# A static scheduler that lengthens both sides of a shared-port overlap, in a kernel of sparse attention and a squared-ReLU layer

## The chip, the cores and the metric

The kernel runs on one core of a Trainium2 chip. The metric is the device time of one execution of the whole program, in microseconds, as the median of several executions; the span of a profile, from its first to its last instruction, is a little shorter.

Five engines of the core work side by side, each in the order of its own instruction list: TensorE (PE, matmuls), VectorE (DVE), ScalarE (ACT), GpSimd (POOL) and SyncE (SP, which here only issues transfers). They wait for each other by semaphores.

## The reference

The reference computes block-sparse attention on 4 batches of 8 heads, 768 positions of 64 features, and then a two-layer feed-forward on the 3072 resulting tokens of 512 features:

```python
scores = (q @ k.T) / sqrt(64)              # per batch and head, 768 x 768
mask   = abs(block_i - block_j) <= 1       # blocks of 32 positions
mask  |= first or last block, as row or as column
mask  |= 3 sampled key blocks for each query block
attn   = softmax(where(mask, scores, -1e9))
x      = (attn @ v), heads side by side     # 3072 tokens x 512
h      = x @ w_in                           # 512 -> 2048
out    = (max(h, 0) ** 2) @ w_out           # 2048 -> 512
```

## The kernel before

The kernel does not write its instructions in a fixed order. It makes a list of tasks, each with the engines that may run it and an estimated duration on each, the tasks it depends on, and the buffers it takes and gives back. A greedy scheduler then walks through estimated time, and each time places the ready task that can start first; ties go to the lower key. What it places becomes the next instruction of that engine. So the estimates decide the order, and the order is fixed before the program runs. On the chip each engine then follows its list, and waits when an input is not there.

```python
LAT = {"PE": 0.23, "DVE": 0.06, "ACT": 0.06, "POOL": 0.08, "SP": 2.0}
SWITCH = 0.1
AHEAD = {"PE": 0.05, "DVE": 0.2, "ACT": 0.25, "POOL": 0.0, "SP": 0.0}
...
def run_schedule(free, bufs, dma_free, mode=128):
    port = {"DVE": (0.0, 0.0), "POOL": (0.0, 0.0)}
    ...
            for e, us in t.engs.items():
                r = max([r0, free[e]] + [seen(d, e) for d in t.deps])
                sw = SWITCH if e == "PE" and t.mode and t.mode != mode else 0.0
                if e == "POOL" or (e == "DVE" and t.port):
                    p0, p1 = port["DVE" if e == "POOL" else "POOL"]
                    us += 0.7 * max(0.0, min(r + us, p1) - max(r, p0))
                if opt is None or r + us + t.bias.get(e, 0.0) < opt[3] - 1e-9:
                    opt = (r + us + sw, r, e, r + us + t.bias.get(e, 0.0))
            found.append((round(opt[1], 4), t.key, t.order, t, opt))
            if t.key < 100:
                urgent[opt[2]] = min(urgent.get(opt[2], 1e9), opt[1])
        best = min((c for c in found if c[1] < 100 or c[0] + AHEAD[c[4][2]] < urgent.get(c[4][2], 1e9)),
                   key=lambda c: c[:3], default=None)
```

`port` holds the last interval of a task on VectorE that uses the SBUF port it shares with GpSimd, and of one on GpSimd. A task that falls into the other engine's interval is made longer by 0.7 of the overlap. The other task, placed already, keeps its length. Tasks with keys under 100 (attention) are urgent; others may start on an engine only if they start by `AHEAD` before the next urgent one.

One attention step is a query tile of 256 positions against two key chunks of 128, for two heads. It is four tasks:

```python
def scores(slots, add, e):      # TensorE, 8 matmuls of 256 columns with 64 rows (two steps: 16)
    ...
                nc.tensor.matmul(ps[:, h, c, :], QK[i][hs, 1, ksl], QK[i][hs, 0, qsl], ...)
def exps(a, e):                 # ScalarE, 128 x 1024, PSUM to SBUF
    A.activation(out=pT, in_=stile.pop(a), func=AF.Exp, scale=scale)
def masks(a, e):                # VectorE, both inputs in SBUF
    V.tensor_tensor(out=pT, in0=pT, in1=m[:, None].broadcast_to([P, 2, 2, QW]), op=AOP.mult)
def values(a, e):               # TensorE, 8 matmuls of 65 columns into the one bank "po"
    ...
def normalize(u, qi, e):        # VectorE, after three steps; then "po" is free again
    V.reciprocal(out=rs, in_=po[:, :, :, D:VW])
    V.tensor_tensor(out=xq, in0=po[:, :, :, 0:D], in1=rs.broadcast_to([P, 2, 2, D]), op=AOP.mult)
```

A score group is four matmuls a step (two heads, two chunks). The first query tile of batch 0 has its mask added by further matmuls; all other steps multiply by a mask `MK` of zeros and ones, which twelve mask tasks on TensorE make at the start. Loads of later batches are cast to bf16 (`cast_qk` on VectorE or GpSimd, `cast_v` mostly on GpSimd).

The feed-forward works on tiles of 256 or 384 tokens:

```python
def hidden(T, f, half, e):      # TensorE, 4 matmuls of 256 or 384 columns for each of 16 f
def relu(T, f, e):              # VectorE or ScalarE, PSUM to SBUF
    if e == "ACT":
        A.activation(out=r, in_=src, func=AF.Relu)
    else:
        V.tensor_scalar(out=r, in0=src, scalar1=0.0, scalar2=None, op0=AOP.max)
def square(T, f, e):            # GpSimd or ScalarE
    if e == "ACT":
        A.activation(out=g, in_=r, func=AF.Square)
    else:
        (G if e == "POOL" else V).tensor_mul(out=g, in0=r, in1=r)
def output(T, ts, part, e):     # TensorE, 16 matmuls of 512 columns for 128 tokens, in 8 parts
    ...
def out_copy(T, ts, e):         # ScalarE or VectorE, PSUM to SBUF, 128 x 512
def store(T, ts, e):            # SyncE
    sy.dma_start(out=ov[T[0], :, T[1] // P + ts, :], in_=ystile.pop((T, ts)))
...
SQ = {256: {"POOL": 0.613, "ACT": 0.39}, 384: {"POOL": 0.826, "ACT": 0.49}}
rr = T_(RELU[w], 200, relu, t, f, deps=[h1], get=[rb], put=[hb], bias={"ACT": 0.4})
sq_of[x] = T_(SQ[w], n_key, square, t, f, deps=[rr], get=[gb], put=[rb], bias={"ACT": 0.5})
```

A `bias` is a penalty in us that keeps a task from an engine unless the other is later by more than that. Hidden and output tasks fill TensorE while attention waits; when attention is over, only they are left.

Of the kernel before, what the change touches and what calls it, by code (L numbers as in the profile page):

```python
# [12 lines left out]
F32 = mybir.dt.float32  # L13
# [6 lines left out]
P = 128  # L20
# [5 lines left out]
def kernel(  # L26
# [11 lines left out]
    nc = tc.nc  # L38
    B, H, S, D = q.shape
# [11 lines left out]
    QW = 256  # L51
# [7 lines left out]
    NRAW, NPB, QC_BUFS, XQ_BUFS = 4, 6, 5, 4  # L59
# [19 lines left out]
    SWITCH = 0.1  # L79
    AHEAD = {"PE": 0.05, "DVE": 0.2, "ACT": 0.25, "POOL": 0.0, "SP": 0.0}  # L80
    LEAD = 12.0
    PACE0, PACE, SINGLE, MASK_AT = 40.0, 1.6, 1, 12.0
# [18 lines left out]
    def run_schedule(free, bufs, dma_free, mode=128):  # L101
        taken = {name: [] for name in bufs}
        port = {"DVE": (0.0, 0.0), "POOL": (0.0, 0.0)}
        waiting = list(tasks)
        ready = []

        def seen(d, eng):
            late = d.late if d.late is not None else (0.0 if d.eng == eng else LAT[d.eng])
            return d.end + late

        while waiting or ready:
# [6 lines left out]
            for t in ready:  # L118
                r0 = t.after
                ok = True  # L120
                cnt = {}
                for b in t.get:
                    held = taken[b.pool]
                    at = len(held) + cnt.get(b.pool, 0) - bufs[b.pool]
                    cnt[b.pool] = cnt.get(b.pool, 0) + 1
                    if at >= 0:
                        if held[at].holds:
                            ok = False
                            break
                        r0 = max(r0, held[at].free)  # L130
                if not ok:
                    continue
                opt = None
                for e, us in t.engs.items():
                    r = max([r0, free[e]] + [seen(d, e) for d in t.deps])
                    sw = SWITCH if e == "PE" and t.mode and t.mode != mode else 0.0
                    if e == "POOL" or (e == "DVE" and t.port):
                        p0, p1 = port["DVE" if e == "POOL" else "POOL"]
                        us += 0.7 * max(0.0, min(r + us, p1) - max(r, p0))
                    if opt is None or r + us + t.bias.get(e, 0.0) < opt[3] - 1e-9:  # L140
                        opt = (r + us + sw, r, e, r + us + t.bias.get(e, 0.0))
                found.append((round(opt[1], 4), t.key, t.order, t, opt))
                if t.key < 100:
                    urgent[opt[2]] = min(urgent.get(opt[2], 1e9), opt[1])
# [7 lines left out]
            if e == "POOL" or (e == "DVE" and t.port):  # L152
                port[e] = (at, end)
            if e == "PE" and t.mode:
                mode = t.mode
# [292 lines left out]
    def y_pool(T, ts):  # L448
        return "h" if T == TILES[-1] and ts % 2 else "y"

    def output(T, ts, part, e):
        if part == 0:
            pool, tag = (ps_h, "h") if y_pool(T, ts) == "h" else (ps_y, "y")
            ytile[T, ts] = pool.tile([P, d_model], F32, name="py", tag=tag)
        py = ytile[T, ts]
        for f in range(part * NF // NY, (part + 1) * NF // NY):
            nc.tensor.matmul(py, gtile[T, f][:, ts * P:(ts + 1) * P], w_out_sb[:, f, :],  # L457
                             start=(f == 0), stop=(f == NF - 1))

    def out_copy(T, ts, e):  # L460
        ys = work.tile([P, d_model], F32, name="ys", tag="ys", bufs=3)
        copy(e, ys, ytile.pop((T, ts)))
        ystile[T, ts] = ys

    def store(T, ts, e):
        sy.dma_start(out=ov[T[0], :, T[1] // P + ts, :], in_=ystile.pop((T, ts)))
# [61 lines left out]
    def attend(group, add):  # L528
# [7 lines left out]
        for a in group:  # L536
# [9 lines left out]
            va = T_(("PE", 0.245), s + 2.2, values, a, deps=[ex] + cv[u] + va_all[-1:],  # L546
# [25 lines left out]
    for us in [range(b * HP, (b + 1) * HP) for b in range(B)]:  # L572
# [3 lines left out]
        if us[0] < HP:  # L576
            for c0, c1, at in ((QW, S, MASK_AT), (0, QW, 26.0)):
# [23 lines left out]
    for k_, T in enumerate(TILES + [None]):  # L601
        hs = [(T, f) for f in range(NF)] if T else []
        ys = [(TILES[k_ - 1], ts, part) for ts in range(TILES[k_ - 1][2] // P) for part in range(NY)] if k_ else []
        both = [((i + 0.5) / len(hs), 0, x) for i, x in enumerate(hs)]
        both += [((i + 0.5) / len(ys), 1, x) for i, x in enumerate(ys)]
        for _, kind, x in sorted(both, key=lambda z: z[:2]):
# [3 lines left out]
            if kind == 0:  # L610
# [10 lines left out]
                rr = T_(RELU[w], 200, relu, t, f, deps=[h1], get=[rb], put=[hb], bias={"ACT": 0.4})  # L621
                sq_of[x] = T_(SQ[w], n_key, square, t, f, deps=[rr], get=[gb], put=[rb], bias={"ACT": 0.5})
            else:
                _, ts, part = x
                fs = range(part * NF // NY, (part + 1) * NF // NY)
                if part == 0:
                    yb = Buf(y_pool(t, ts))
                last_ts = ts == w // P - 1
                yy = T_(("PE", 0.432), n_key, output, t, ts, part,
                        deps=[sq_of[t, f] for f in fs] + [wl[NWP + f * NWP // NF] for f in fs] + ([yprev] if part else []),  # L630
                        get=[] if part else [yb], put=[gbuf[t, f] for f in fs] if last_ts else [], mode=128)
                yprev = yy
                if part == NY - 1:
                    sb = Buf("ys")
                    yc = T_({"ACT": 0.585, "DVE": 0.68}, 150, out_copy, t, ts, deps=[yy], get=[sb], put=[yb])
                    T_(("SP", 0.2), 0, store, t, ts, deps=[yc], put=[sb], late=2.0)

    run_schedule({"PE": 5.6, "DVE": 5.6, "ACT": 5.5, "POOL": 5.2, "SP": 12.0},
                 {"ps": 2, "po": 1, "h": 2, "y": 1, "pT": PT_BUFS, "r": R_BUFS, "g": G_BUFS, "ys": 3,
# [31 lines left out]
```

The softmax here doesn't subtract the row's maximum and nothing guards it: scores larger than these inputs give would overflow.

## Time and profile before

The median of three runs is 281.56 us (281.35 to 282.2). The profiled execution has a span of 279.6 us with TensorE's clock at full speed throughout.

| Group (line of the kernel) | Engine | Count | Busy, us | Mean of one, ns |
|---|---|---|---|---|
| hidden matmuls (L427) | TensorE | 576 | 107.8 | 308 |
| output matmuls (L457) | TensorE | 384 | 103.5 | 379 |
| values matmuls (L382) | TensorE | 1152 | 56.5 | 194 |
| scores matmuls (L349) | TensorE | 576 | 46.5 | 272 |
| exponentials (L359) | ScalarE | 144 | 139.2 | 1021 |
| rectifiers (L434) | ScalarE | 64 | 27.3 | 451 |
| squares (L443) | ScalarE | 37 | 18.1 | 489 |
| mask products (L366) | VectorE | 132 | 105.1 | 815 |
| rectifiers (L436) | VectorE | 80 | 41.9 | 525 |
| squares (L445) | GpSimd | 107 | 94.5 | 889 |
| copies of the output (L170) | ScalarE | 21 | 12.3 | 586 |

In lines of the profile, L followed by a number is a line of the kernel. A line of waits reads: who waited, for whom, then the total in us, how often, and the longest. In a line of the order of time the start comes first, then the duration, both in us, then engine, line, operation, output and inputs, and how many instructions were merged; in brackets stands how long the engine had been idle and what ended it. Matmul durations are pipelined and their ends are modelled.

### The profile page before, as it was taken

The numbers are of one execution on the slowest core, as the hardware profiler recorded it, in microseconds if no ns is written. First come the engines' busy times: TensorE is split into PE (matmuls) and PEld (weight loads), VectorE is DVE, ScalarE is ACT, GpSimd is POOL, SyncE is SP. The second block draws the span as 40 slices with busy tenths as digits, with TensorE's granted clock in tenths as the row PEclk, the third lists the DMA queues.
The fourth block names the chain that finished last, engine by engine and source line by source line (L and its number), as shares of the span: only waits on it lengthen the run. The fifth ranks groups of instructions, "written<-read, shape, count | busy, mean of one in ns | idle before, by whom it ended". The sixth has DMA issues, their size and how long they took to land.

```text
span 279.6 us, 7039 instructions
## 1 busy us (share of the span) xinstructions
PE 267.9 (96%) x2834; PEld 155.6 (56%) x2834; DVE 200.4 (72%) x379; ACT 196.5 (70%) x281; POOL 122.1 (44%) x151
## 2 busy tenths in 40 slices
PE   7888899999999998999999999999999999999994
PEld 2565566566666554555555555555556555555541
DVE  6776889898988779986877888877868744344400
ACT  4689889899899799798988889889789501001011
POOL 4570358576434359752114443211120366666610
PEclk9999999999999999999999999999999999999999
DMA  7999997999933784794106314321011010111112
GB/s 249 378 228 207 269 277 239 195 285 258 357 65 83 237 193 120 213 191 106 56 12 115 81 45 111 70 59 49 19 51 56 12 47 38 40 39 38 40 74 76
DMA packets 50379, 36.89 MB, mean 132 GB/s; under 512 B 30891, under 2 KB 47275, under 8 KB 50347
## 3 DMA queue, kind: packets, MB, share of 16 engines
q1 hardware_dynamic: 44762, 30.29, 40.7%
q0 software_dynamic: 4224, 4.19, 9.0%
q10 hardware_dynamic: 1360, 1.97, 2.1%
q8 instruction: 22, 0.36, 0.6%
q14 instruction: 11, 0.08, 0.1%
HBM read 27.26 MB, written 6.29 MB: 120 GB/s over the span
## 4 chain that ended last, share of the span: by engine, by line
PE 78%; DVE 15%; ACT 4%; issue 2%; ACTq 0%; DVEq 0%
PE py L457 27%; PE ph L427 25%; PE po L382 12%; PE ps L349 11%; DVE pT L366 8%; DVE qc L172 3%; ACT pT L359 2%; DVE xq L391 2%; PE junk L213 2%; DVE rs L389 1%; DVE QK L172 1%; PE pt L301 1%; PE ps L353 0%; DVE r L436 0%; DVE xT L172 0%
## 5 line engine op out<-in xcount | busy, mean ns | idle before, releaser
L445 POOL TENSOR_TENSOR g<-r 128x384 bf16<-128x384 f32 (+1 forms) x107 | 94.5, 889 | 128.8 <-DVE r L436 93.0
L359 ACT ACTIVATE pT<-ps 128x1024 bf16<-128x1024 f32 x144 | 139.2, 1021 | 10.8 <-PE ps L349 7.6
L366 DVE TENSOR_TENSOR pT<-pT,MK 128x1024 bf16<-128x1024 bf16 x132 | 105.1, 815 | 9.0 <-ACT pT L359 8.7
L427 PE MATMUL ph<-xT,w_in_sb 128*128 128x384 bf16 (+1 forms) x576 | 107.8, 308 | 0.0
L457 PE MATMUL py<-w_out_sb,g 128*128 128x512 bf16 x384 | 103.5, 379 | 0.0
L427 PEld LDWEIGHTS <-w_in_sb 128*128 128x128 bf16 x576 | 51.1, 97 | 33.3 <-issue 3.4
L436 DVE TENSOR_SCALAR r<-ph 128x384 f32<-128x384 f32 (+1 forms) x80 | 41.9, 525 | 32.9 <-PE ph L427 22.2
L382 PEld LDWEIGHTS <-pT 128*128 128x128 bf16 x1152 | 45.8, 98 | 28.9 <-DVE pT L366 10.9
L382 PE MATMUL po<-VT,pT 128*128 128x65 bf16 x1152 | 56.5, 194 | 3.2 <-DVE pT L366 1.2
L457 PEld LDWEIGHTS <-g 128*128 128x128 bf16 x384 | 34.4, 98 | 25.7 <-issue 1.5
L170 ACT COPY ys<-py 128x512 f32<-128x512 f32 x21 | 12.3, 586 | 50.2 <-PE py L457 50.0
L349 PE MATMUL ps<-QK 64*128 64x256 bf16 x576 | 46.5, 272 | 1.0 <-ACT pT L359 0.8
L349 PEld LDWEIGHTS <-QK 64*128 64x128 bf16 x576 | 22.9, 94 | 21.2 <-issue 17.0
L434 ACT ACTIVATE r<-ph 128x384 f32<-128x384 f32 (+1 forms) x64 | 27.3, 451 | 6.7 <-PE ph L427 6.2
L443 ACT ACTIVATE g<-r 128x384 bf16<-128x384 f32 (+1 forms) x37 | 18.1, 489 | 6.4 <-DVE r L436 5.8
L391 DVE TENSOR_TENSOR xq<-po,rs 128x256 bf16<-128x256 f32 x48 | 20.4, 424 | 1.7
L172 POOL CAST VT<-vs 128x768 bf16<-128x768 f32 x15 | 14.8, 986 | 12.7 <-PE po L382 7.9
L389 DVE RECIPROCAL rs<-po 128x4 f32<-128x4 f32 x48 | 8.6, 179 | 14.9 <-PE po L382 14.7
L172 DVE CAST qc<-qs 128x768 bf16<-128x768 f32 (+2 forms) x15 | 10.2, 683 | 0.7 <-DMA qs<-in_q_dram 0.7
L172 DVE CAST qc<-ks 128x768 bf16<-128x768 f32 x14 | 10.5, 747 | 0.0
L353 PE MATMUL ps<-R,oh 64*128 64x256 bf16 x48 | 5.9, 269 | 0.0
L213 PE MATMUL junk<-warm 128*128 128x512 bf16 x12 | 4.4, 542 | 1.5 <-DVE warm L205 1.5
(52 smaller groups left out, 60.2 us busy)
## 6 DMA issues: line engine op xcount, KB each, us to landing
out_dram<-ys SPq DMA_DIRECT2D x24, 256.0 KB, 2.0
vs<-in_v_dram SPq DMA_DIRECT2D x15, 384.0 KB, 6.6
qs<-in_q_dram SPq DMA_DIRECT2D x14, 384.0 KB, 4.3
ks<-in_k_dram SPq DMA_DIRECT2D x14, 384.0 KB, 6.2
w_in_sb<-in_moe_w_in_dram POOLq DMA_DIRECT2D x4, 512.0 KB, 9.6
w_out_sb<-in_moe_w_out_dram POOLq DMA_DIRECT2D x4, 512.0 KB, 20.1
ks<-in_k_dram ACTq DMA_DIRECT2D x2, 384.0 KB, 6.2
qs<-in_q_dram ACTq DMA_DIRECT2D x2, 384.0 KB, 4.8
```

The costliest lines, as they stand in the source:

```text
L172: (V if e == "DVE" else G).tensor_copy(out=out, in_=in_)
L349: nc.tensor.matmul(ps[:, h, c, :], QK[i][hs, 1, ksl], QK[i][hs, 0, qsl], start=c == 0, stop=not add, skip_group_check=True)
L359: A.activation(out=pT, in_=stile.pop(a), func=AF.Exp, scale=scale)
L366: V.tensor_tensor(out=pT, in0=pT, in1=m[:, None].broadcast_to([P, 2, 2, QW]), op=AOP.mult)
L382: nc.tensor.matmul(po[:, qc, h, :], pT[:, h, c, qc * P:(qc + 1) * P], VT[i][:, h, n, 0:VW], start=(n == 0 and qc == 0 and h == 0), stop=n ...
L391: V.tensor_tensor(out=xq, in0=po[:, :, :, 0:D], in1=rs.broadcast_to([P, 2, 2, D]), op=AOP.mult)
L427: nc.tensor.matmul(ph, w_in_sb[:, kc, f * P:(f + 1) * P], xT[b][:, kc, c0:c0 + w], start=(kc == 0), stop=(kc == KM - 1))
L434: A.activation(out=r, in_=src, func=AF.Relu)
L436: V.tensor_scalar(out=r, in0=src, scalar1=0.0, scalar2=None, op0=AOP.max)
L443: A.activation(out=g, in_=r, func=AF.Square)
L445: (G if e == "POOL" else V).tensor_mul(out=g, in0=r, in1=r)
L457: nc.tensor.matmul(py, gtile[T, f][:, ts * P:(ts + 1) * P], w_out_sb[:, f, :], start=(f == 0), stop=(f == NF - 1))
```

## The change

The scheduler's model of the shared port becomes two-sided: where a VectorE task and a GpSimd task overlap, the one placed second is lengthened by 0.6 of the overlap, and so is the one placed first, along with the time when its engine and its buffers are free. Inputs that TensorE gets from other engines count as 0.1 us later than estimated (`SLACK`), so that its order leaves room for estimates that are off. The bias against ScalarE falls for squares and rises for rectifiers. Values are ranked 0.5 later. Mask tiles for the first query tile may start at 38 instead of 26 us. Pacing, `AHEAD` and the lead of loads are set anew. The output of the last 128 tokens is computed, copied and stored in two halves of 256 columns, so that the first half leaves while the second is computed.

The diff, without moved blank lines:

```diff
--- before.py
+++ after.py
@@ -56,7 +56,7 @@
     VW = D + 1
     N_WARM = 12
-    NRAW, NPB, QC_BUFS, XQ_BUFS = 4, 6, 5, 4
+    NRAW, NPB, QC_BUFS, XQ_BUFS, YS_BUFS = 4, 6, 5, 4, 3
     PT_BUFS, R_BUFS, G_BUFS, XT_BUFS = 6, 4, 2 * NF + 2, 3
     consts = ctx.enter_context(tc.tile_pool(name="consts", bufs=1))
     ld = ctx.enter_context(tc.tile_pool(name="ld", bufs=NRAW))
@@ -76,10 +76,10 @@
     tasks = []
     LAT = {"PE": 0.23, "DVE": 0.06, "ACT": 0.06, "POOL": 0.08, "SP": 2.0}
     OVER = {"PE": 0.0, "DVE": 0.08, "ACT": 0.09, "POOL": 0.03, "SP": 0.0}
-    SWITCH = 0.1
-    AHEAD = {"PE": 0.05, "DVE": 0.2, "ACT": 0.25, "POOL": 0.0, "SP": 0.0}
-    LEAD = 12.0
-    PACE0, PACE, SINGLE, MASK_AT = 40.0, 1.6, 1, 12.0
+    SWITCH, SHARE, SLACK = 0.096, 0.6, 0.1
+    AHEAD = {"PE": 0, "DVE": 0, "ACT": 0.2, "POOL": 0.0, "SP": 0.0}
+    LEAD = 14
+    PACE0, PACE, SINGLE, MASK_AT = 44, 1.313, 1, 12.0
     class Buf:
         def __init__(self, pool):
@@ -101,12 +101,13 @@
     def run_schedule(free, bufs, dma_free, mode=128):
         taken = {name: [] for name in bufs}
         port = {"DVE": (0.0, 0.0), "POOL": (0.0, 0.0)}
+        last = {"DVE": None, "POOL": None}
         waiting = list(tasks)
         ready = []
         def seen(d, eng):
             late = d.late if d.late is not None else (0.0 if d.eng == eng else LAT[d.eng])
-            return d.end + late
+            return d.end + late + (SLACK if eng == "PE" and d.eng != "PE" else 0.0)
         while waiting or ready:
             now = [t for t in waiting if all(d.end is not None for d in t.deps)]
@@ -136,7 +137,7 @@
                     sw = SWITCH if e == "PE" and t.mode and t.mode != mode else 0.0
                     if e == "POOL" or (e == "DVE" and t.port):
                         p0, p1 = port["DVE" if e == "POOL" else "POOL"]
-                        us += 0.7 * max(0.0, min(r + us, p1) - max(r, p0))
+                        us += SHARE * max(0.0, min(r + us, p1) - max(r, p0))
                     if opt is None or r + us + t.bias.get(e, 0.0) < opt[3] - 1e-9:
                         opt = (r + us + sw, r, e, r + us + t.bias.get(e, 0.0))
                 found.append((round(opt[1], 4), t.key, t.order, t, opt))
@@ -151,6 +152,15 @@
             t.end, free[e] = end, end - OVER[e]
             if e == "POOL" or (e == "DVE" and t.port):
                 port[e] = (at, end)
+                o = "DVE" if e == "POOL" else "POOL"
+                more = SHARE * max(0.0, min(end, port[o][1]) - max(at, port[o][0]))
+                if more and last[o]:
+                    last[o].end += more
+                    for b in last[o].put:
+                        b.free = max(b.free, last[o].end + LAT[o])
+                    free[o] += more
+                    port[o] = (port[o][0], port[o][1] + more)
+                last[e] = t
             if e == "PE" and t.mode:
                 mode = t.mode
             if t.dma:
@@ -445,25 +455,35 @@
             (G if e == "POOL" else V).tensor_mul(out=g, in0=r, in1=r)
         gtile[T, f] = g
-    def y_pool(T, ts):
-        return "h" if T == TILES[-1] and ts % 2 else "y"
-    def output(T, ts, part, e):
+    WHOLE = (0, d_model)
+    HALVES = ((0, d_model // 2), (d_model // 2, d_model))
+    def y_tiles(T):
+        n = T[2] // P
+        ys = [(ts, WHOLE) for ts in range(n)]
+        return ys[:-1] + [(n - 1, cs) for cs in HALVES] if T == TILES[-1] else ys
+    def y_pool(T, i):
+        return "h" if T == TILES[-1] and i % 2 else "y"
+    def output(T, i, ts, cs, part, e):
         if part == 0:
-            pool, tag = (ps_h, "h") if y_pool(T, ts) == "h" else (ps_y, "y")
-            ytile[T, ts] = pool.tile([P, d_model], F32, name="py", tag=tag)
-        py = ytile[T, ts]
+            pool, tag = (ps_h, "h") if y_pool(T, i) == "h" else (ps_y, "y")
+            ytile[T, i] = pool.tile([P, d_model], F32, name="py", tag=tag)[:, 0:cs[1] - cs[0]]
         for f in range(part * NF // NY, (part + 1) * NF // NY):
-            nc.tensor.matmul(py, gtile[T, f][:, ts * P:(ts + 1) * P], w_out_sb[:, f, :],
+            nc.tensor.matmul(ytile[T, i], gtile[T, f][:, ts * P:(ts + 1) * P], w_out_sb[:, f, cs[0]:cs[1]],
                              start=(f == 0), stop=(f == NF - 1))
-    def out_copy(T, ts, e):
-        ys = work.tile([P, d_model], F32, name="ys", tag="ys", bufs=3)
-        copy(e, ys, ytile.pop((T, ts)))
-        ystile[T, ts] = ys
-    def store(T, ts, e):
-        sy.dma_start(out=ov[T[0], :, T[1] // P + ts, :], in_=ystile.pop((T, ts)))
+    def out_copy(T, i, cs, e):
+        ys = work.tile([P, d_model], F32, name="ys", tag="ys", bufs=YS_BUFS)[:, 0:cs[1] - cs[0]]
+        copy(e, ys, ytile.pop((T, i)))
+        ystile[T, i] = ys
+    def store(T, i, ts, cs, e):
+        sy.dma_start(out=ov[T[0], :, T[1] // P + ts, cs[0]:cs[1]], in_=ystile.pop((T, i)))
@@ -543,7 +563,7 @@
                 ex = T_(("DVE", 0.68), s - 1, masks, a, deps=[ex, mk[cp * 2, qi], mk[cp * 2 + 1, qi]], port=True)
             if cp == 0:
                 ob[u, qi] = Buf("po")
-            va = T_(("PE", 0.245), s + 2.2, values, a, deps=[ex] + cv[u] + va_all[-1:],
+            va = T_(("PE", 0.245), s + 2.7, values, a, deps=[ex] + cv[u] + va_all[-1:],
                     get=[] if cp else [ob[u, qi]], put=[pt], mode=128)
             va_all.append(va)
             va_of[u].append(va)
@@ -574,7 +594,7 @@
             prepare(u)
         mine = [a for a in order if a[0] in us]
         if us[0] < HP:
-            for c0, c1, at in ((QW, S, MASK_AT), (0, QW, 26.0)):
+            for c0, c1, at in ((QW, S, MASK_AT), (0, QW, 38.0)):
                 for n in range(NCH):
                     mb, w = Buf("h"), (c1 - c0) / 512
                     t = T_(("PE", 0.216 * w), 2 * n + (2 if c0 else 30), mask_tile, n, c0, c1, get=[mb], mode=128, after=at, deps=mr)
@@ -600,7 +620,7 @@
     gbuf, hbuf = {}, {}
     for k_, T in enumerate(TILES + [None]):
         hs = [(T, f) for f in range(NF)] if T else []
-        ys = [(TILES[k_ - 1], ts, part) for ts in range(TILES[k_ - 1][2] // P) for part in range(NY)] if k_ else []
+        ys = [(TILES[k_ - 1], i, part) for i in range(len(y_tiles(TILES[k_ - 1]))) for part in range(NY)] if k_ else []
         both = [((i + 0.5) / len(hs), 0, x) for i, x in enumerate(hs)]
         both += [((i + 0.5) / len(ys), 1, x) for i, x in enumerate(ys)]
         for _, kind, x in sorted(both, key=lambda z: z[:2]):
@@ -618,25 +638,27 @@
                         get=[hb], mode=128)
                 h1 = T_(("PE", HID[w]), n_key - 0.6, hidden, t, f, 1, deps=[h0],
                         put=[xb[b]] if last_use else [], mode=128)
-                rr = T_(RELU[w], 200, relu, t, f, deps=[h1], get=[rb], put=[hb], bias={"ACT": 0.4})
-                sq_of[x] = T_(SQ[w], n_key, square, t, f, deps=[rr], get=[gb], put=[rb], bias={"ACT": 0.5})
+                rr = T_(RELU[w], 200, relu, t, f, deps=[h1], get=[rb], put=[hb], bias={"ACT": 0.5})
+                sq_of[x] = T_(SQ[w], n_key, square, t, f, deps=[rr], get=[gb], put=[rb], bias={"ACT": 0.2})
             else:
-                _, ts, part = x
+                _, i, part = x
+                ts, cs = y_tiles(t)[i]
+                n = (cs[1] - cs[0]) / d_model
                 fs = range(part * NF // NY, (part + 1) * NF // NY)
                 if part == 0:
-                    yb = Buf(y_pool(t, ts))
-                last_ts = ts == w // P - 1
-                yy = T_(("PE", 0.432), n_key, output, t, ts, part,
+                    yb = Buf(y_pool(t, i))
+                last_i = i == len(y_tiles(t)) - 1
+                yy = T_(("PE", 0.432 * n), n_key, output, t, i, ts, cs, part,
                         deps=[sq_of[t, f] for f in fs] + [wl[NWP + f * NWP // NF] for f in fs] + ([yprev] if part else []),
-                        get=[] if part else [yb], put=[gbuf[t, f] for f in fs] if last_ts else [], mode=128)
+                        get=[] if part else [yb], put=[gbuf[t, f] for f in fs] if last_i else [], mode=128)
                 yprev = yy
                 if part == NY - 1:
                     sb = Buf("ys")
-                    yc = T_({"ACT": 0.585, "DVE": 0.68}, 150, out_copy, t, ts, deps=[yy], get=[sb], put=[yb])
-                    T_(("SP", 0.2), 0, store, t, ts, deps=[yc], put=[sb], late=2.0)
+                    yc = T_({"ACT": 0.22 + 0.365 * n, "DVE": 0.15 + 0.53 * n}, 150, out_copy, t, i, cs, deps=[yy], get=[sb], put=[yb])
+                    T_(("SP", 0.2), 0, store, t, i, ts, cs, deps=[yc], put=[sb], late=2.0)
     run_schedule({"PE": 5.6, "DVE": 5.6, "ACT": 5.5, "POOL": 5.2, "SP": 12.0},
-                 {"ps": 2, "po": 1, "h": 2, "y": 1, "pT": PT_BUFS, "r": R_BUFS, "g": G_BUFS, "ys": 3,
+                 {"ps": 2, "po": 1, "h": 2, "y": 1, "pT": PT_BUFS, "r": R_BUFS, "g": G_BUFS, "ys": YS_BUFS,
                   "qc": QC_BUFS, "xq": XQ_BUFS, "xT": XT_BUFS}, dma_free=15.2)
```

## The prediction

> **What bounds the kernel now.** I read the page's first two parts, then busy time by stretches of 20 us, then the waits of TensorE and its stream in order of time. The page says that TensorE is the wall:
>
> ```profile
> span 279.6 us, 7039 instructions
> PE 267.9 (96%) x2834; PEld 155.6 (56%) x2834; DVE 200.4 (72%) x379; ACT 196.5 (70%) x281; POOL 122.1 (44%) x151
> PE 78%; DVE 15%; ACT 4%; issue 2%; ACTq 0%; DVEq 0%
> ```
>
> The busy share of TensorE overstates the work, because each group of matmuls is shown with its pipeline depth. Four hidden matmuls are shown as 0.81 us, yet the chain that ended last moves on after 0.65 us. So I took 0.165 us off the shown end of each group and measured to the next start. Summed over the span this gives 10.2 us in gaps over 0.15 us; smaller gaps come to about 1 us in each 20 us of attention and to nothing after 220 us. The stretches show where the large gaps lie:
>
> ```profile
> core 0: us, PE busy (x) PEld busy (x) DVE busy (x) ACT busy (x) POOL busy (x), PEclk, DMA share, GB/s
> 20.00:40.00 20.00, 18.09 (x257) 11.89 (x256) 15.38 (x35) 17.90 (x26) 4.89 (x7) 1.00 1.20 240
> 100.00:120.00 20.00, 18.53 (x216) 10.38 (x210) 18.16 (x27) 17.04 (x25) 16.34 (x15) 1.00 0.74 181
> 140.00:160.00 20.00, 20.00 (x232) 11.68 (x229) 15.52 (x32) 17.84 (x24) 6.84 (x7) 1.00 0.35 64
> 240.00:260.00 20.00, 20.00 (x109) 10.55 (x108) 8.37 (x15) 1.75 (x3) 12.46 (x16) 1.00 0.08 30
> ```
>
> At 100 to 120 us GpSimd is busy for 16.3 us, VectorE for 18.2 us, and TensorE loses time. At 140 to 160 us GpSimd is busy for 6.8 us and TensorE loses nothing. The gaps over 0.15 us are: 3.6 us before 25 us, 1.93 us from 26 to 30 us, 2.26 us from 41 to 68 us, 2.05 us from 111 to 121 us, and 0.34 us in all later attention. The waits name the releasers:
>
> ```profile
> PE po L382 <- DVE pT L366: 1.2, 4, 0.4
> PE po L382 <- DVE xq L391: 1.1, 1, 1.1
> PE pt L301 <- DVE QK L172: 1.1, 1, 1.1
> PE po L398 <- DVE xq L391: 1.0, 2, 0.5
> PE ps L349 <- ACT pT L359: 0.8, 2, 0.4
> PE pk L275 <- DVE MK L283: 0.3, 1, 0.3
> ```
>
> Nearly all are VectorE being late. The longest, in order of time (start, duration, engine, line, operation), shows how it comes about:
>
> ```profile
> 107.54 2.54 DVE L366 TENSOR_TENSOR pT<-pT,MK 128x1024 bf16<-128x1024 bf16 x2
> 109.48 1.28 POOL L172 CAST VT<-vs 128x768 bf16<-128x768 f32 x1
> 110.01 1.17 DVE L172 CAST qc<-qs 128x768 bf16<-128x768 f32 x1
> 111.31 0.42 DVE L391 TENSOR_TENSOR xq<-po,rs 128x256 bf16<-128x256 f32 x1
> 111.79 0.42 PE L382 MATMUL po<-VT,pT 128*128 128x65 bf16 x8 [1.11 <-DVE xq L391]
> ```
>
> The two mask products took 2.54 us beside GpSimd squares. Two of them at 183.75 us, with GpSimd idle, took 1.28 us. The cast took 1.17 us against 0.55 us for a lone one at 96.87 us. VectorE therefore reached the normalisation late, the single bank for attention output was not free, and the next values matmul waited 1.11 us. GpSimd is stretched as well: a square of 384 columns takes 0.82 us after 220 us, where VectorE only evacuates PSUM, and 1.20 us at 105 to 121 us. The old scheduler lengthens only the operation that it places second; the first keeps its short time.
>
> **What the Trainium skill says.** "SBUF — State Buffer", section "Who interferes with whom", says that VectorE and GpSimd share one pair of SBUF ports, that a VectorE operation with two SBUF inputs collides with a GpSimd operation that reads SBUF, and that this is an exclusive lock in which the later one blocks. The trace agrees on which operations collide. On the form it differs: both sides stretch (0.64 to 1.27 us for a mask product, 0.82 to 1.20 us for a square), which is what the new model assumes. "Perfetto Trace Analysis", section "Optimizing Scalar/DVE Operations", warns that moving work between these two engines may not help because of that port; the change moves it to ScalarE instead. "TensorEngine Tiling (Array Packing)", section "Key Properties", says that a change of tiling mode drains TensorE. The trace agrees: scores run in a 64-row mode, and around each group stands a gap of about 0.1 us. "DMA: Bandwidth & Descriptors", section "Anatomy of one DMA — SWDGE (gpsimd) path", gives about 2.0 us of fixed cost a transfer; the output stores here, from another queue, land in a median of 2.0 us.
>
> **The change part by part.** The instruction orders of both builds give counts; durations are from the trace of before.
>
> 1. *TensorE work.* The same matmuls, except that 16 output matmuls of 512 columns become 32 of 256. The chain gives 0.216 us for one of the first (0.86 for 4), and 0.109 us for 256 columns (hidden, 0.87 for 8): 32 x 0.109 - 16 x 0.216 = +0.03 us. Mode changes go from 153 to 155: +0.2 us at 0.1 each.
>
> 2. *Squares.* GpSimd's fall from 107 to 59, ScalarE's rise from 37 to 85. ScalarE's rectifiers fall from 64 to 48, VectorE's rise from 80 to 96. Some 30 of the ScalarE squares stand after its last exponential, where ScalarE was nearly idle (1.75 us of 20). In that tail TensorE was already dense, so moving them brings nothing. Inside attention ScalarE gets about 18 squares at 0.5 us and loses 16 rectifiers at 0.45: +2 us over some 190 us. VectorE gets 18 more rectifiers there: +10 us. From it go two casts (1.5 us), and stretching: 132 products x (0.815 - 0.64) = 23 us of stretch now stands beside some 82 us of GpSimd work. With about 14 us of squares fewer and two casts more on GpSimd, some 71 us remain, so about 3 us of stretch goes. VectorE ends about 5 us fuller over 190 us, which is tight but fits its 15.5 to 18 us of 20.
>
> 3. *Order.* This is the gain. The values task is ranked 0.5 later, TensorE tasks get 0.1 us of slack, and both sides of an overlap are lengthened. I counted, in both orders, how much TensorE work stands between a scores group and its values group; exponential and mask must fit in it. Leaving out the first 12 groups, those with under 2.6 us between fall from 25 to 6, and in the last 108 groups from 19 to 2. The gaps from 41 to 68 us and 111 to 121 us are just this. Of 2.26 I expect 1.5 back, of 2.05 + 0.34 some 1.9.
>
> 4. *Second half of the mask* released at 38 instead of 26 us. At 26 to 30 us six mask matmuls and their evacuations, three of them on VectorE, compete with the first mask products; hidden matmuls now stand there. Of 1.93 us I expect 1.2 back. The 3.6 us before 25 us hang on loads and on chains of one attention head with no other work at hand: 0.2 back.
>
> 5. *Last tokens in halves.* The end of before is:
>
> ```profile
> 265.72 10.31 PE L457 MATMUL py<-w_out_sb,g 128*128 128x512 bf16 x47
> 276.11 0.58 ACT L170 COPY ys<-py 128x512 f32<-128x512 f32 x1 [2.87 <-PE py L457]
> ```
>
> The first half's copy and store lie beside the second half's matmuls. On the path, a copy of 256 columns replaces one of 512. ScalarE's rectifier of that shape takes 0.40 us, so 0.18 us goes. Half the bytes in the last store spare perhaps 0.1 us of the 2.0, which is mostly fixed. Together 0.3 us.
>
> Sum: 1.5 + 1.9 + 1.2 + 0.2 + 0.3 = 5.1 us back; 0.2 for mode changes and 0.5 for new waits of a fuller VectorE and ScalarE go off: 4.4 us. 281.56 - 4.4 = about 277.2 us.
>
> **The rivals.** *ScalarE or VectorE becomes the bound in attention.* ScalarE is already busy 17 to 18 us of 20, and squares now stand between exponentials, so scores may wait for their PSUM buffer. For it: the trace has such a wait (0.8 us in all). Against it: ScalarE's sum there hardly moves. The gain would shrink to 1 or 2 us: 279.5 to 280.5. *The handover of the single output bank takes over.* TensorE work between one tile's last values and the next tile's first: under 1.1 us in 7 handovers of batches 1 to 3 before, 10 after, and two of batch 0 have only 0.66. If each cost 0.2 to 0.6 us, 2 to 3 us would be lost: about 279.5. *Weights.* Hidden and output work starts some 1.5 to 2 us earlier. The gate transfers show that the second quarter of the output weights was there at 35.0 and the last at 42.0 us. Counting along the new order, the matmuls that need them come at about 36.5 and 46 us; a slip would cost at most a microsecond. *The model fits almost perfectly.* Then nearly all 10.2 us but the start go, to about 273.5 us.
>
> **Range and chances.** No TensorE work is removed, so the gaps and the tail cap the gain near 10.5 us (271). 2% is 5.6 us, to 275.9; that needs more than half the gap time back, including some of the start. The rivals cost 2 to 3 us and more probably trim the gain than turn it. Range 275.0 to 279.7; faster 0.20, same 0.77, slower 0.03.
>
> **What would show it.** Right: no wait of values on a normalisation over 0.5 us from 100 to 125 us; mask products under 0.80 us in the mean; GpSimd near 75 us busy; gaps over 0.15 us summing to 5 to 6 us; TensorE dense after 220 us as before; the last copy near 0.40 us. Wrong: waits of scores on exponentials or of values on masks that sum to more than 3 us between 60 and 220 us, or output matmuls waiting for squares on ScalarE.

## The result, and the profile after

The changed kernel takes 277.17 us (median of 4, 276.55 to 278.07), the kernel before 281.88 us. The ratio is 0.9836 with a 95% interval of 0.980 to 0.9871: 4.7 us are gone. That is 1.6%, less than the 2% from which the prediction would call it faster.

From the page of the changed kernel, the span, the engines and the chain that ended last:

```profile
span 275.2 us, 7001 instructions
PE 263.5 (96%) x2812; PEld 156.7 (57%) x2850; DVE 198.0 (72%) x392; ACT 212.0 (77%) x315; POOL 77.3 (28%) x105
PE 87%; DVE 4%; ACT 3%; DMA 2%; issue 2%; POOL 1%; POOLq 0%; ACTq 0%
```

VectorE's share of the chain has fallen from 15% to 4%. The busy time of TensorE can't be compared: there are 2850 weight loads, but 2812 matmuls, so 38 records of matmuls are missing (all of output matmuls, about 0.22 us each). In the order of time they look like gaps of 0.22 us beside an output matmul; I took 0.216 us off each of these.

The groups that the change was to move (line, engine, operation, count, then busy us and mean ns):

```profile
L376 DVE TENSOR_TENSOR pT<-pT,MK 128x1024 bf16<-128x1024 bf16 x132 | 98.8, 769 | 10.5 <-ACT pT L369 10.3
L455 POOL TENSOR_TENSOR g<-r 128x256 bf16<-128x256 f32 (+1 forms) x59 | 50.0, 853 | 164.5 <-DVE r L446 134.6
L446 DVE TENSOR_SCALAR r<-ph 128x384 f32<-128x384 f32 (+1 forms) x96 | 49.6, 519 | 28.5 <-PE ph L437 27.2
L453 ACT ACTIVATE g<-r 128x384 bf16<-128x384 f32 (+1 forms) x85 | 42.3, 501 | 29.2 <-DVE r L446 28.5
```

The counts are those of the orders. Mask products have a mean of 769 ns instead of 815. The waits of TensorE that are left:

```profile
PE pt L311 <- DVE QK L182: 0.9, 1, 0.9
PE po L408 <- DVE xq L401: 0.9, 2, 0.7
PE py L477 <- POOL g L455: 0.9, 1, 0.9
PE po L392 <- DVE xT L182: 0.7, 2, 0.4
PE po L392 <- ACT pT L369: 0.3, 1, 0.3
PE pk L285 <- DVE QK L182: 0.2, 1, 0.2
```

Waits of values on mask products (1.2 us) and on a normalisation (1.1 us) are gone. A new one is an output matmul that waits 0.86 us for a square on GpSimd, at 51.7 us.

The same reckoning of gaps as in the prediction (0.165 us off each shown end, only gaps over 0.15 us), by stretch:

| Stretch, us | Before | After |
|---|---|---|
| up to 30 | 5.5 | 4.5 |
| 30 to 60 | 2.0 | 1.8 |
| 60 to 100 | 0.3 | 0 |
| 100 to 125 | 2.05 | 0 |
| 125 to the end | 0.35 | 0 |
| sum | 10.2 | 6.3 |

So 3.9 of the 4.4 us between the two spans are large gaps of TensorE. The stretch that was worst before, in the columns of the table of stretches (TensorE, weight loads, VectorE, ScalarE, GpSimd):

```profile
100.00:120.00 20.00, 19.84 (x236) 11.69 (x238) 17.02 (x31) 18.75 (x29) 7.91 (x10) 1.00 0.68 169
```

GpSimd has half the work of before here (7.9 instead of 16.3 us), and the 0.16 us that TensorE seems to lose stand beside missing records (236 matmuls, 238 weight loads). This line can't tell whether the cause is that there is less to collide with, or that the order reckons with collisions. The experiments are for that.

### The profile page after: what moved, and what is told of

The parts are those of the page before. It is cut to its first block, busy times and chain, and to the rows that moved or that the text cites. A ratio compares the mean times of both kernels' runs of the same rounds, so it can differ in the third digit from the quotient of the medians.

```text
span 275.2 us, 7001 instructions
## 1 busy us (share of the span) xinstructions
PE 263.5 (96%) x2812; PEld 156.7 (57%) x2850; DVE 198.0 (72%) x392; ACT 212.0 (77%) x315; POOL 77.3 (28%) x105
## 4 chain that ended last, share of the span: by engine, by line
PE 87%; DVE 4%; ACT 3%; DMA 2%; issue 2%; POOL 1%; POOLq 0%; ACTq 0%
PE ph L437 28%; PE py L477 28%; PE po L392 14%; PE ps L359 12%; DMA vs<-in_v_dram 2%; ACT pT L369 2%; PE junk L223 2%; DVE pT L376 1%; PE pt L311 1%; DVE r L446 1%; POOL g L455 1%; DVE QK L182 1%; PE po L408 1%; PE ps L363 0%; ACT MK L291 0%
## 5 line engine op out<-in xcount | busy, mean ns | idle before, releaser
L376 DVE TENSOR_TENSOR pT<-pT,MK 128x1024 bf16<-128x1024 bf16 x132 | 98.8, 769 | 10.5 <-ACT pT L369 10.3
L477 PE MATMUL py<-w_out_sb,g 128*128 128x512 bf16 (+1 forms) x362 | 96.2, 369 | 2.5 <-POOL g L455 0.9
L455 POOL TENSOR_TENSOR g<-r 128x256 bf16<-128x256 f32 (+1 forms) x59 | 50.0, 853 | 164.5 <-DVE r L446 134.6
L446 DVE TENSOR_SCALAR r<-ph 128x384 f32<-128x384 f32 (+1 forms) x96 | 49.6, 519 | 28.5 <-PE ph L437 27.2
L453 ACT ACTIVATE g<-r 128x384 bf16<-128x384 f32 (+1 forms) x85 | 42.3, 501 | 29.2 <-DVE r L446 28.5
L392 PE MATMUL po<-VT,pT 128*128 128x65 bf16 x1152 | 53.9, 194 | 1.5 <-DVE xT L182 0.7
L477 PEld LDWEIGHTS <-g 128*128 128x128 bf16 x400 | 36.3, 97 | 24.7 <-POOL g L455 1.2
L444 ACT ACTIVATE r<-ph 128x384 f32<-128x384 f32 (+1 forms) x48 | 21.0, 445 | 5.3 <-PE ph L437 4.7
L180 ACT COPY ys<-py 128x512 f32<-128x512 f32 (+1 forms) x21 | 11.9, 565 | 11.7 <-PE py L477 11.7
L182 DVE CAST qc<-qs 128x768 bf16<-128x768 f32 (+2 forms) x13 | 8.6, 666 | 0.8 <-DMA qs<-in_q_dram 0.8
```

The source lines that it names most:

```text
L182: (V if e == "DVE" else G).tensor_copy(out=out, in_=in_)
L392: nc.tensor.matmul(po[:, qc, h, :], pT[:, h, c, qc * P:(qc + 1) * P], VT[i][:, h, n, 0:VW], start=(n == 0 and qc == 0 and h == 0), stop=n ...
L477: nc.tensor.matmul(ytile[T, i], gtile[T, f][:, ts * P:(ts + 1) * P], w_out_sb[:, f, cs[0]:cs[1]], start=(f == 0), stop=(f == NF - 1))
```

## The experiments

Three theories were put against each other. **A**: the gain comes from the room that the order leaves between scores and values (slack, later rank). **B**: it comes from the squares that left GpSimd, so that less collides on the shared port. **C**: it comes from the two-sided lengthening, because the order then doesn't expect VectorE to be done earlier than it is.

All ratios are against the kernel before on the same chip. Each variant is a new order of thousands of tasks, so differences of under a microsecond between two variants are not read as the effect of what was edited. A profile's start also varies: with the same lists, the first copy of transposed queries began at 7.2 us in the profile of the changed kernel and at 8.0 us in that of its variant without squares on GpSimd. The matmul that makes the first mask rows started 0.8 us later there; why stays open. So medians are compared, not spans.

### The parts alone, on the kernel before

**The two-sided model alone.** The edit, cut to its core:

```diff
-SWITCH = 0.1
+SWITCH, SHARE = 0.1, 0.6
-                        us += 0.7 * max(0.0, min(r + us, p1) - max(r, p0))
+                        us += SHARE * max(0.0, min(r + us, p1) - max(r, p0))
...
+                more = SHARE * max(0.0, min(end, port[o][1]) - max(at, port[o][0]))
+                if more and last[o]:
+                    last[o].end += more
...
+                    free[o] += more
```

> The kernel before with nothing but the two-sided lengthening by 0.6. 106 squares on GpSimd, 15 tight values groups of the last 108 (19 before). Theory A (room between scores and values): under 1.5 us gained, above 280. Theory B (squares off GpSimd): nothing gained. Theory C (the model): 2.5 us or more gained, 279 or less, and the 1.1 us wait near 112 us is gone.

Measured: 278.27 us, ratio 0.9871 (0.9844 to 0.9897), 3.7 us gained. The squares on GpSimd are as many as before, and the mask products are as slow as before:

```profile
L455 POOL TENSOR_TENSOR g<-r 128x384 bf16<-128x384 f32 (+1 forms) x106 | 96.5, 918 | 121.9 <-DVE r L446 82.5
L376 DVE TENSOR_TENSOR pT<-pT,MK 128x1024 bf16<-128x1024 bf16 x132 | 105.2, 815 | 8.9 <-ACT pT L369 8.2
```

And the stretch from 100 to 120 us, with GpSimd nearly as busy as before (16.34 us):

```profile
100.00:120.00 20.00, 20.00 (x239) 11.81 (x238) 16.82 (x28) 19.27 (x31) 15.85 (x16) 1.00 0.75 185
```

TensorE loses nothing. The collisions are still there, mean 815 ns in both, but the order is another. C foretold this, A and B did not: 15 of the last 108 values groups still have under 2.6 us of TensorE work ahead.

Lengthening both sides isn't a closer model of an overlap, since on the chip only the operation that starts later waits (last section). It is a more cautious one. Each kernel's scheduler, run by itself, gives the estimates that it worked with: for a mask product 0.790 us in the mean before, where 0.815 was measured, and 0.855 us here, where 0.815 was measured again. Worked out like this, the mean estimate is longer than the measured mean (by 0.01 to 0.05 us) in every order made with the two-sided model, and shorter (by 0.02 to 0.03 us) in every order made without it (the two runs without squares left aside). Single mask products are missed by more than before: by 0.15 us in the mean here, by 0.09 us before. This fits C, but it is no test of it. Whether the lengthening has to be on both sides, or a plainly longer estimate for VectorE would do as well, was not run and stays open.

**Slack and rank alone.**

```diff
-            return d.end + late
+            return d.end + late + (0.1 if eng == "PE" and d.eng != "PE" else 0.0)
-            va = T_(("PE", 0.245), s + 2.2, values, ...
+            va = T_(("PE", 0.245), s + 2.7, values, ...
```

> The kernel before with nothing but 0.1 us of slack and values ranked 0.5 later. 99 squares on GpSimd, 7 tight values groups of the last 108. Theory A: 2 to 3.5 us gained, about 278.8. Theory B: under 1 us gained. Theory C: under 1 us gained.

Measured: 279.82 us, 0.9925 (0.9897 to 0.9953), 2.1 us gained. The lower end of what A said, and more than C said. Room by slack is thus worth something by itself, though the two gains (3.7 and 2.1 us) can't be added: the whole change gains 4.7. Fewer tight groups (7) than with the two-sided model, and less gain, so the count that I had used in the prediction doesn't rank the orders.

**Biases alone.**

```diff
-rr = T_(RELU[w], 200, relu, ..., bias={"ACT": 0.4})
-sq_of[x] = T_(SQ[w], n_key, square, ..., bias={"ACT": 0.5})
+rr = T_(RELU[w], 200, relu, ..., bias={"ACT": 0.5})
+sq_of[x] = T_(SQ[w], n_key, square, ..., bias={"ACT": 0.2})
```

> The kernel before with nothing but the new biases: 53 squares on GpSimd, 91 on ScalarE, 17 tight values groups of the last 108. Theory A: under 1 us gained. Theory B: 2.5 us or more gained, 279 or less. Theory C: under 1 us gained.

Measured: 282.44 us, 1.0015 (1.0004 to 1.0025), 0.4 us lost by the ratio. Halving the squares on GpSimd brought nothing, which B can't explain. The mask products are shorter, and the waits for them twice as long as before (2.6 instead of 1.2 us):

```profile
L366 DVE TENSOR_TENSOR pT<-pT,MK 128x1024 bf16<-128x1024 bf16 x132 | 100.6, 775 | 11.0 <-ACT pT L359 10.3
PE po L382 <- DVE pT L366: 2.6, 7, 0.5
```

Pacing, `AHEAD` and the lead of loads were never changed alone. The two-sided model gains 3.7 of the 4.7 us without them; what they add is not known.

### What the collision costs

Here the order is held, and the collision is taken away: GpSimd fills a square's tile with a constant, which reads nothing, and squares only 16 columns, so that it still waits for the same input. The computation of the squares on GpSimd is left out.

```diff
-            (G if e == "POOL" else V).tensor_mul(out=g, in0=r, in1=r)
+            G.memset(g, 0.25)
+            G.tensor_mul(out=g[:, 0:16], in0=r[:, 0:16], in1=r[:, 0:16])
```

**On the kernel before.**

> The kernel before in its own order, but a square on GpSimd is left out: it fills the tile with a constant, which reads no SBUF, and squares 16 of its columns alone. The output is not the reference's. GpSimd's large reads are gone beside the mask products. If the clash on the port is what makes VectorE late: mask products fall from 0.815 to under 0.70 us in the mean, the large gaps after 40 us (4.7 us) fall under 1.5 us, and the time falls by 2.5 to 4 us. If VectorE is late because of its own load and the tight order, the mask products get shorter but less than 1.5 us is gained.

Measured: 276.92 us, 0.9818 (0.9789 to 0.9846), 5.0 us gained, more than foretold. The mask products come to the foretold 0.70 us:

```profile
L366 DVE TENSOR_TENSOR pT<-pT,MK 128x1024 bf16<-128x1024 bf16 x132 | 91.0, 701 | 13.4 <-ACT pT L359 12.7
```

GpSimd is not idle here (13.4 us of the stretch from 100 to 120 us, before 16.3), but filling reads no SBUF, and the products come down from 815 to 701 ns. That GpSimd is done sooner is no rival here: before, VectorE waits for a square on GpSimd only from 227 us on, where TensorE is dense. Since the lists are the same, each weight load has a counterpart before, and the starts can be compared one by one. At 28 us this run is 0.2 us ahead; at 48 us 1.5; at 100 us 1.6; at 123 us 3.6; at the end 4.25. These are the stretches where TensorE had its gaps, and after 40 us no gap is left over 0.15 us, except one that the substitute itself makes (an output matmul waits 1.5 us for GpSimd at 52 us). So nearly all that TensorE lost after 30 us was due to reads of GpSimd that stretched VectorE.

**On the changed kernel.**

> The changed kernel in its own order, with the squares on GpSimd left out (a constant is filled in, 16 columns are squared), as was done with the kernel before. The output is not the reference's. It says what the clash on the port still costs. If the two-sided model has made room for it: under 1.2 us gained, 276 or more (the wait of an output matmul on GpSimd at 51.7 us, 0.86 us, may go). If the gain is only that fewer squares clash, about half of them being left: 2 us or more gained, 275 or less.

Measured: 277.25 us, 0.982 (0.9793 to 0.9846), not to be told from the changed kernel (0.9836). By the starts of weight loads 0.8 us is gained between 29 and 57 us (the wait for GpSimd at 51.7 us and a smaller one), and less than 0.1 us in all the time after. The 59 squares that GpSimd has left still collide in the changed kernel (mask products take 769 ns there, 700 here), yet they cost nothing after 57 us. In the old order the collision is worth 5 us, in the new one under 1. This shows that the new order has room for it; as the new order has the slack and fewer squares too, it doesn't tell C from A and B.

### The parts taken out, on the changed kernel

**Only the second is lengthened.** `more` is set to zero; the share stays at 0.6.

> The changed kernel without the lengthening of the operation placed first (only the second is lengthened, by 0.6). 57 squares on GpSimd, 2 tight values groups of the last 108. If the two-sided model itself is the gain (theory C): 2 us or more lost, 279.2 or more. By theories A and B: within 0.7 us of 277.2, since both the room and the squares are as in the changed kernel.

Measured: 280.13 us, 0.9942 (0.9912 to 0.9971). The kernel with the last tokens whole, on the same chip, has 0.985 and 278.03 us, so 2.6 us are lost by the ratios and 2.1 us by the medians. That is what C said, by the second figure narrowly. There are no more squares on GpSimd and no slower mask products than in the changed kernel (59 and 769 ns):

```profile
L376 DVE TENSOR_TENSOR pT<-pT,MK 128x1024 bf16<-128x1024 bf16 x132 | 98.4, 760 | 10.5 <-ACT pT L369 10.2
L455 POOL TENSOR_TENSOR g<-r 128x384 bf16<-128x384 f32 (+1 forms) x57 | 49.8, 876 | 169.6 <-DVE r L446 144.5
```

TensorE's large gaps sum to 9.0 us instead of 6.3: 3.2 instead of 1.8 us between 30 and 60 us, and 1.0 instead of none after. What is lost is thus lost by the order, not by more collisions.

**No slack, old rank.**

> The changed kernel without the 0.1 us of slack and with values at their old rank (2.2). Squares stay as in the changed kernel (59 on GpSimd); 10 values groups of the last 108 have under 2.6 us of work ahead. Theory A (room in the order): 1 to 2 us lost, about 278.5, with waits of values on mask products. Theory B (fewer squares on GpSimd): nothing lost, 277.2.

Measured: 279.08 us, 0.9891 (0.9861 to 0.9921), 1.2 us lost against the same neighbour (0.985). A part of the gain, smaller than that of the two-sided model.

**Old biases.**

> The changed kernel with the old biases, so that squares go back: 102 on GpSimd, 42 on ScalarE. In its order no values group of the last 108 has under 2.6 us of TensorE work ahead of it (2 in the changed kernel, 19 in the kernel before). Theory A, the gain comes from an order with more room between scores and values: it stays within 1 us of 277.2. Theory B, the gain comes from taking squares off the port that GpSimd shares with VectorE: at least 2.5 us are lost, 279.7 or more, and values wait for VectorE again between 60 and 220 us.

Measured: 279.46 us, 0.9904 (0.9871 to 0.9936), 1.5 us lost against the neighbour, between what A and B said. After 62 us only one gap over 0.15 us is left (0.4 us), with 102 squares on GpSimd; what is lost lies mostly between 41 and 62 us, where a values group waits 0.6 us for a mask product. So this order is worse, and of the waits for mask products that B foretold between 60 and 220 us only two are there, 0.5 us together. Inconclusive alone; the last run below shows an order in which nearly as many squares on GpSimd don't cost this.

**Second half of the mask at 26 us.**

> The changed kernel with the second half of the mask released at 26 us, as before. By my sum 1.2 us are lost, as gaps of TensorE between 26 and 31 us (1.24 us before in the three gaps next to mask tasks, none now). If the mask work only moves its gaps, the loss is under 0.5 us, and the gap at 41 us (0.52 us) goes.

Measured: 277.56 us, 0.9836 (0.982 to 0.9852), the same ratio as the changed kernel has, though not measured beside it. Its gaps at 29 and 30 us come back (0.39 and 0.50 us, both waits for mask products), and the one at 41 us goes: the mask work only moves its gaps.

**The last tokens whole.** `HALVES` is one piece.

> The changed kernel with the last 128 tokens in one piece. By my sum 0.3 us lost (277.5); by the profile after, in which the tail from TensorE's end to the end of the span is 3.5 us as before, 0.1 us or nothing.

Measured: 278.03 us, 0.985 (0.9811 to 0.989), not to be told from 0.9836. The tail from TensorE's end to the end of the span is 3.61 us here and 3.54 with halves.

### Where the gain of the halves went, and other constants

The end of the changed kernel, in the order of time (start, duration):

```profile
270.04 0.37 ACT L180 COPY ys<-py 128x256 f32<-128x256 f32 x1 [1.21 <-PE py L477]
271.78 0.37 ACT L180 COPY ys<-py 128x256 f32<-128x256 f32 x1 [1.37 <-PE py L477]
```

The copy takes 0.37 us instead of 0.58, and the last store lands 1.70 us after its issue instead of 2.00: 0.5 us saved, but the span ends 1.36 us after the last landing, before 0.92. The trace shows SyncE at the end of the program waiting for eight semaphores of transfers in turn, about 0.063 us each. Transfers get these semaphores in rotation. With 24 stores the last one fell on the eighth, so the other seven were already checked; with 25 it falls on the first, and seven checks come after its landing: 7 x 0.063 = 0.44 us. To test this, the first two stores are made one, which turns the rotation back by one:

```diff
+        if T == TILES[0]:
+            sy.dma_start(out=ov[T[0], :, 0:2, :], in_=ystile.pop(T))
+            return
         sy.dma_start(out=ov[T[0], :, T[1] // P + ts, cs[0]:cs[1]], in_=ystile.pop((T, i)))
```

> The changed kernel with one transfer fewer: the first two stores of the output are one. The lists of TensorE, VectorE, ScalarE and GpSimd are the same. The semaphores of the hardware queues' transfers are given out in turn, eight of them, so the last store falls on the eighth (which SyncE waits for last at the end of the program) instead of the first. If the seven waits after the last landing are what ate the gain of the halves: the span ends 0.44 us sooner after the last landing (0.92 us instead of 1.36), TensorE's end to the end of the span 3.1 us instead of 3.54, and the time about 276.8. If the end of the program is bound by something else, the tail stays at 3.5 us.

Measured: the tail is 3.08 us, with 0.91 us after the last landing, so the cause is shown. The time, 277.9 us and 0.9847 (0.9834 to 0.9861), doesn't show the 0.46 us; it is smaller than what starts and chips differ by, and this profile has its first gaps later and larger.

**Other constants for the same model.** Nothing is changed but numbers: pacing, leads, ranks and biases, together with the turned rotation.

```diff
-    AHEAD = {"PE": 0, "DVE": 0, "ACT": 0.2, "POOL": 0.0, "SP": 0.0}
-    LEAD = 14
-    PACE0, PACE, SINGLE, MASK_AT = 44, 1.313, 1, 12.0
+    AHEAD = {"PE": 0.073, "DVE": 0.024, "ACT": 0.139, "POOL": 0.0, "SP": 0.0}
+    LEAD = 10.00
+    PACE0, PACE, SINGLE, MASK_AT = 41.15, 0.974, 1, 10.20
...
-                sq_of[x] = T_(SQ[w], n_key, square, ..., bias={"ACT": 0.2})
+                sq_of[x] = T_(SQ[w], n_key, square, ..., bias={"ACT": 0.349})
```

> The changed kernel with the one transfer fewer and with other constants of the scheduler: pacing 41.15 and 0.974 instead of 44 and 1.313, lead 10, second half of the mask at 45.4 us, values ranked 2.83, bias of squares against ScalarE 0.349 instead of 0.2, of casts of q and k against GpSimd 0.98. It puts 94 squares on GpSimd (59 in the changed kernel) and 50 on ScalarE. If the two-sided model makes the clash harmless: 275 to 276.5 in spite of the squares. If squares on GpSimd are harmful in themselves: 278.5 or more.

Measured: 276.95 us, 0.9807 (0.9794 to 0.982), 0.45 us above the range that was foretold for a harmless clash and far below the other one. On the same chip the changed kernel with the turned rotation has 0.9847 (0.9834 to 0.9861) and 277.9 us, so this is about 1 us better than that one, with intervals apart. The changed kernel itself was not run beside it; its interval (0.980 to 0.9871) overlaps, so it isn't shown that this version is faster. It has 94 squares on GpSimd instead of 59, and slower mask products (792 instead of 769 ns):

```profile
L455 POOL TENSOR_TENSOR g<-r 128x384 bf16<-128x384 f32 (+1 forms) x94 | 83.4, 891 | 129.9 <-DVE r L446 91.9
L376 DVE TENSOR_TENSOR pT<-pT,MK 128x1024 bf16<-128x1024 bf16 x132 | 101.5, 792 | 7.1 <-ACT pT L369 6.4
```

After 60 us its gaps over 0.15 us sum to under 0.5 us. So with the two-sided model 94 squares on GpSimd cost nothing that can be seen. The other constants changed too, so this run doesn't say what each of them does.

## Why the prediction was right, point by point

The time came out as predicted, 277.2 and 277.17 us, and it came from where it was said, from VectorE being late less often. But the sum has errors that cancel, and the weight in step 3 was wrong. That the number fits to 0.1 us is luck.

*What bounds the kernel.* Right. Of 10.2 us of large gaps 3.9 came back, of the 4.4 us between the spans; 6.3 us are left, where 5 to 6 were named as the sign of being right.

*The form of the clash.* Wrong. The prediction reads the trace as differing from an exclusive lock, because both sides stretch. The trace agrees with such a lock: in each overlap only the operation that starts later waits, and where both engines have work in a row each is the later one in turn (last section). So the new model is not nearer to the chip in form.

*Step 1, TensorE work.* Nothing contradicts +0.2 us; it is too small to be seen.

*Step 2, squares.* Counts right, GpSimd at 77.3 us (foretold near 75), mask products under 0.80 us. VectorE was to get 5 us fuller; its sum fell by 2.4 us, from 200.4 to 198.0. The stretch that goes was mis-sized: 132 x (815 - 769) = 6.1 us instead of 3. The lone product was mis-sized as well. I had halved a merged pair (0.64 us); with no read of GpSimd beside it a product takes 0.683 us (55 of the 132 before), with one beside it throughout 1.014 us in the mean (16 of them).

*Step 3, order.* From 100 us on 2.4 us came back where 1.9 were expected; from 41 to 68 us, 0.4 of 2.26 where 1.5 were expected. What came in there were two new waits that I had not placed: 0.52 us for the evacuation of the transposed attention output, and 0.81 us for the square on GpSimd, which stood between two casts. The total of this step held, its reasoning only in part. I rested it on the count of tight values groups. The two-sided model alone leaves 15 of 19 such groups and gains 3.7 us; slack and rank alone leave 7 and gain 2.1. So what counted is less the room by that count than that VectorE is done no later than the order expects; by the estimates above, the two-sided model gets there by being cautious. I had named the clash as the cause of the long wait at 111 us; that was right, and it should have carried the step.

*Step 4, mask.* Of 1.4 us that were expected up to 30 us, 1.0 is gone in the profile; but releasing the mask at 26 us again costs nothing (0.9836 in both). The term is worth nothing that can be seen: its gaps move to 40 us.

*Step 5, halves.* Expected 0.3 us, found 0.07. Copy (0.21 for 0.18) and store (0.30 for 0.1) gave more than expected, and the rotation of semaphores took 0.44 us back, which the prediction didn't have.

*The rivals.* None came in force. Scores wait for ScalarE for less than 0.2 us in all, although it is busy 212 us; no values group waits on a normalisation in batches 1 to 3; no wait for weights shows. The perfect fit failed at the start: 4.5 of the remaining 6.3 us lie before 30 us, where attention of one head after the other has no other work beside it, as the prediction said.

## What to carry to other kernels

If a static order decides what an engine does next, an operation that is stretched by a neighbour costs its stretch only where the order left no time for it. So let the estimates of both engines hold the stretch, rather too much of it than too little (as the two-sided model did here), before moving work away. Removing the collision with the order held says what it is worth (5.0 us here), and doing it again after the change says what is left (under 1 us). At the end of a program, count what comes after the last landing too.

## What the runs showed of the hardware

In each overlap on the shared port the operation that starts later waits, and the earlier one keeps its length. From the kernel before, in the order of time:

```profile
144.11 0.68 DVE L366 TENSOR_TENSOR pT<-pT,MK 128x1024 bf16<-128x1024 bf16 x1
144.27 1.20 POOL L445 TENSOR_TENSOR g<-r 128x384 bf16<-128x384 f32 x1 [7.25 <-DVE r L436]
144.95 1.07 DVE L366 TENSOR_TENSOR pT<-pT,MK 128x1024 bf16<-128x1024 bf16 x1 [0.16 <-ACT pT L359]
```

The first mask product takes its 0.68 us. The square starts while 0.52 us of it are left, and takes 1.20 us, 0.38 us longer than a lone one (0.826 us). The second product starts while 0.52 us of the square are left, and takes 0.39 us longer. Over this whole trace, 27 mask products started first and had a GpSimd operation that reads SBUF come in later: they take 0.68 us in the mean, like lone ones. Another 51 started while such an operation ran: 50 of them are longer by the time that it still had to run less 0.14 us, to within 0.04 us (and not at all where that is under 0.14 us). All 49 squares and 9 casts on GpSimd that started during a mask product or a cast on VectorE follow the same sum. Where both engines have work in a row, both slow down: a mask product takes up to 1.33 us, a square of 384 columns up to 1.27 us, a cast of values on GpSimd up to 1.31 instead of 0.82 us.

VectorE operations that read PSUM pay nothing: the normalisation, with one input in PSUM, takes 0.424 us with and without GpSimd beside it, the rectifier of 384 columns 0.554 and 0.555 us. A fill on GpSimd doesn't stretch the mask product: in the old order without squares, 17 products beside a fill alone take 0.686 us, 55 with nothing beside them 0.684 us. And the eight checks of transfers at the end of the program, 0.063 us each, were not expected to be on the path at all.
